# Output tiles in three parts, half-done products of w3 and w_out, a drain that can be split over two engines, and a new written order (attention and maxout FFN, one core)

## The chip, the core and the metric

The kernel runs on one core of one Trainium2 chip. The metric is the device time of one execution in microseconds; three runs of the kernel before gave 163.84, 164.56 and 164.87 us, the median is 164.56 us. The core has a tensor engine for matmuls (PE in the profile; PEld is its weight load), a vector engine (DVE), a scalar engine (ACT), GpSimd (POOL), and SyncE (SP), which here only issues output DMAs. Each engine runs its own instructions strictly in the order in which the program issued them; engines wait for one another by semaphores.

## What is computed

There are 8 batches of 8 heads, 576 rows and 64 columns a head; 32 memory slots per head. In short:

```python
a      = softmax(phi, axis=rows)                      # per head, 576 x 32
k_m    = a.T @ k ; v_m = a.T @ v                      # 32 x 64 per head
attn   = softmax(q @ k_m.T / 8, axis=slots)           # 576 x 32
x      = concat over heads of attn @ v_m              # 4608 x 512
h      = max(x @ w1, x @ w2, x @ w3)                  # 4608 x 768
out    = h @ w_out                                    # 4608 x 512, float32
```

## The kernel before, in words

The kernel never forms x. Per batch it folds the value slots into the weights: with d1 = w1 - w3 and d2 = w2 - w3, `h = x@w3 + max(x@d1, x@d2, 0)`, and since x = attn @ v_m, the products v_m @ d1, v_m @ d2 and v_m @ (w3 @ w_out) are made first (tile `wp`, 1536 columns, and tile `wp3`, 512 columns; line 433 and on, `fold`). Then `ffn1` (L461) makes attn @ wp in chunks of 128 hidden columns, and `ffn2` (L510) adds, for each output tile of 128 rows, six matmuls of hidden chunks against `w_out` (L532) and two matmuls of attn against wp3, the slots' values (L541; for t = 4, a tile of 64 rows of each of two batches, four half-size ones, L522).

All work is written out by hand: the string at L621 is a list of tokens `letter number @ batch`, and `issue` (L586) calls one function for each. An engine's queue is the order in which these tokens give it instructions. The letters that matter here:

- loads, all issued by POOL: L0 phi, L1 keys, L2 values, L3 queries of a batch; H0 to H3 the half loads of batch 0; Y0, Y1, Y2 the weights w1, w2, w3, and Y3 w_out. `r0`, `r1` pack keys and values side by side (POOL copies, L104); `G` makes POOL wait for a load.
- softmax over rows: E (ACT exponent), B (matmuls 64x32, L254), N (DVE, L274 to L288), K (transposes L303, then a drain). Batches 0 and 1 do keys and values apart (B0, B1 and so on).
- scores: Q (DVE transposes of q, L318, in two halves), S (matmuls 32x32, L338, then two ACT exponents, L347), then the softmax over slots on DVE and POOL: a (transpose L392), s (sum L400), c (reciprocal L409), m (POOL multiply L414), X (transpose back L422). Number 0 and 1 are two halves of the heads. Batch 0 does it with matmuls instead (M, R, X).
- D: fold, D0 D1 D2 the three column blocks of wp, D3 wp3; batch 0 has D0, D1, D2, D4, whose blocks differ (512, 256, 256 and 512 columns, `FIRST` at L211). V subtracts w3 from w1 and w2 in place on DVE (L219) once batch 0's folds have read them.
- F: even numbers are the d1 half of a chunk, drained with a relu to tile `h` (ACT L178 or DVE L182); odd ones are the d2 half, joined by a DVE max into tile `hT` (L484).
- P: the first three hidden matmuls of an output tile (`ffn2_head`, L495); T: the rest of it, its drain to tile `ot` and its output DMA.
- W, O: transposes of w3, and the rows of w3 @ w_out (six matmuls each, L200, drained to tile `w3o`). Z: matmuls on zeros that keep PE busy.

A drain is the copy of a finished PSUM result to SBUF. `evacuate` (L174) takes the engine from the table `EVAC` ("a" ACT, "v" DVE, by letter and number), and a `!` behind a token swaps it. PSUM is one tile of 8 banks; `one_bank` and `two_banks` (L156, L159) take the next digit of a second hand-written string (L149), which gives the first bank. A matmul into a bank waits until the bank's last reader is done.

Of the kernel before, what the change touches and what calls it, by code (L numbers as in the profile page):

```python
# [15 lines left out]
def kernel(  # L16
# [124 lines left out]
    for i in range(P // M):  # L141
# [4 lines left out]
    banks = iter(  # L146
        "".join(
            """
            60606026024506010445024062406246024602434403424206026420462406240723043240604602  # L149
            46026402645260502624620640264024601642102461462624604624260462045260024062404206  # L150
            12640264014206502402605220462406420462036040432402677670
            """.split()
        )
    )
# [1 line left out]
    def one_bank():  # L156
        return psum[:, int(next(banks))]
# [13 lines left out]

    EVAC = {"D": "avaaa", "T": "vavav", "K": "v", "W": "vvv", "O": "aaaa", "F": "aaaaaa"}

    def evacuate(kind, n, swap, out_, in_, relu=False):  # L174

        if (EVAC[kind][n] == "a") != swap:
            if relu:
                nc.scalar.activation(out=out_, in_=in_, func=AF.Relu)  # L178
            else:
                nc.scalar.copy(out=out_, in_=in_)  # L180
        elif relu:
            nc.vector.tensor_scalar_max(out=out_, in0=in_, scalar1=0.0)  # L182
        else:
            nc.vector.tensor_copy(out=out_, in_=in_)  # L184

    def w3_t(f2, swap):
# [7 lines left out]
                )  # L194
        evacuate("W", f2, swap, w3T[:, 2 * f2 : 2 * f2 + 2], pt)

    def w3_o(j, swap):
        po = one_bank()
        for f in range(FT):
            nc.tensor.matmul(  # L200
                po,
                lhsT=w3T[:, f, j, :],
                rhs=wo_sb[:, f, :],
                start=(f == 0),
                stop=(f == FT - 1),
            )
        evacuate("O", j, swap, w3o[:, j, :], po)
# [115 lines left out]
    attns = {}  # L323
# [168 lines left out]

    heads = {}

    def ffn2_head(b, t):  # L495

        hT = hts[b // 2]
        c0 = (b % 2) * (S + HP) + t * P
        po = heads[b, t] = one_bank()
        for n in range(HEAD):  # L500
            fc = fts[b][n]
            nc.tensor.matmul(  # L502
                po,
                lhsT=hT[:, fc, c0 : c0 + P],
                rhs=wo_sb[:, fc, :],
                start=(n == 0),
                stop=False,
            )

    def ffn2(b, t, swap):  # L510


        hT, attn = hts[b // 2], attns[b // 2]
        c0 = S - HP if t == 4 else (b % 2) * (S + HP) + t * P
        if b == B - 1 and t == 3:
            return ffn2_last(b, c0)
        po = heads[b, t] if (b, t) in heads else one_bank()

        if t == 4:
            for g in range(NG):  # L520
                for u in range(2):
                    nc.tensor.matmul(  # L522
                        po[HP * u : HP * (u + 1)],
                        lhsT=attn[:, g, c0 + HP * u : c0 + HP * (u + 1)],
                        rhs=wp3s[b - 1 + u][:, g, :],
                        start=(g == 0),
                        stop=False,
                        tile_position=(0, HP * u),
                    )
        for n in range(HEAD if (b, t) in heads else 0, FT):  # L530
            fc = fts[b][n]
            nc.tensor.matmul(  # L532
                po,
                lhsT=hT[:, fc, c0 : c0 + P],
                rhs=wo_sb[:, fc, :],
                start=(n == 0 and t < 4),
                stop=(n == FT - 1 and t == 4),
            )
        if t < 4:
            for g in range(NG):  # L540
                nc.tensor.matmul(  # L541
                    po,
                    lhsT=attn[:, g, c0 : c0 + P],
                    rhs=wp3s[b][:, g, :],
                    start=False,
                    stop=(g == NG - 1),
                )
        ot = opool.tile([P, DM], FP32, name="ot")
        r0 = (b // 2) * 2 * S + c0
        rows = out[r0 : r0 + P, :]  # L550
        evacuate("T", t, swap, ot, po)
        nc.sync.dma_start(out=rows, in_=ot)
# [66 lines left out]


    for w in """  # L621
        E@0 H0@0 H2@0 L3@0 Z25@0 B0@0 I@0 N0@0 Z2@0 K0@0! Q0@0 Q1@0 Z9@0 S@0 Z2@0 M0@0 M1@0
        R0@0 Y2@0 G0@0 R1@0 W0@0 Y3@0 W1@0 W2@0 Z6@0 O1@0 H3@0 O3@0 O2@0 H1@0 X1@0 B1@0 X0@0
        N1@0 K1@0 O0@0 Y0@0 D1@0! D0@0! D3@0 F8@0 F10@0 F2@0 V0@0 F6@0 F0@0! Y1@0 D2@0 L0@1
        V2@0 L1@1 D4@0 V1@0 L3@1 F4@0 F3@0 L2@1 L1@2 F1@0 L2@2 F7@0 F5@0 F9@0 F11@0 P0@0 E@1
        B0@1 N0@1 T3@0 K0@1! Q0@1 Q1@1 L0@2 T0@0! S@1 L3@2 P1@0 V4@0 B1@1 a0@1 T1@0 s0@1 L3@3
        N1@1 c0@1 L2@3 a1@1 s1@1 K1@1 c1@1 m0@1 P2@0 X0@1 D1@1 D0@1 m1@1 D2@1 X1@1 T2@0! L1@3
        r0@2 F2@1! F10@1 F0@1! F4@1 F8@1 F5@1 r1@2 F6@1 L0@3 E@2 F9@1 F11@1 L0@4 L1@4 F1@1 F7@1
        P2@1 F3@1 B@2 N@2 D3@1 P3@1 P0@1 K@2! Q0@2 Q1@2 T0@1! S@2 a0@2 s0@2 c0@2 T4@1! m0@2
        a1@2 s1@2 c1@2 T2@1! D2@2 Q1@3 D0@2 D1@2! T3@1 m1@2 T1@1 X1@2 r1@3 L3@4 L2@4 X0@2 L2@5  # L630
        Q0@3 F4@2 F6@2 F0@2 F8@2 F7@2 r0@3 F1@2 F10@2 F5@2 E@3 F9@2 F11@2 F2@2 B@3 D3@2 N@3
        F3@2 L0@5 P3@2 K@3 P0@2 L1@5 S@3 T0@2 a0@3 r0@4 s0@3 c0@3 a1@3 s1@3 P2@2 m0@3 c1@3 D2@3
        m1@3 D1@3! L3@5 D0@3 T3@2! Q1@4 X0@3 X1@3 T2@2! Q0@4 T1@2 F10@3! r1@4 F2@3 F11@3 F6@3
        F8@3! F3@3 E@4 F4@3 F9@3 F5@3 F0@3 F7@3 B@4 D3@3 N@4 F1@3 P1@3 K@4 L1@6 L0@6 T1@3! r1@5
        E@5 S@4 D2@4 L2@6 a0@4 T4@3! r0@5 s0@4 L0@7 a1@4 P0@3 D1@4! B@5 s1@4 c1@4 D0@4 L1@7
        c0@4 Q1@5 m1@4 T0@3! N@5 Q0@5 K@5 P2@3 L2@7 X1@4 m0@4 S@5 X0@4 T2@3! F0@4 F2@4 a0@5
        F4@4! F6@4 r1@6 a1@5 P3@3 L3@6 D1@5! r0@6 D3@4 s1@5 D3@5! T3@3 F10@4 s0@5 c1@5 F3@4
        F8@4 c0@5 F11@4 F1@4 F7@4 F5@4 F9@4 m0@5 P1@4 P0@4 E@6 D0@5 m1@5 X0@5 B@6 D2@5 X1@5
        T0@4 T1@4 N@6 F6@5 F0@5 F7@5 F1@5 F4@5! Q0@6 F2@5 r0@7 F10@5 r1@7 T3@4! Q1@6 F5@5 F8@5!
        E@7 K@6! F9@5 T2@4! F3@5 S@6 F11@5 a1@6 B@7 L3@7 D2@6 N@7 a0@6 D0@6 T4@5! s0@6 K@7 Q1@7  # L640
        P0@5 s1@6 D1@7! D3@7 c1@6 c0@6 D0@7 Q0@7 m1@6 T0@5! m0@6 P1@5 S@7 T1@5 X1@6 a0@7 a1@7
        P3@5 X0@6 D2@7 D1@6! s0@7 c0@7 D3@6 s1@7 T3@5! m0@7 c1@7 F6@6 P2@5 m1@7 X0@7 X1@7 F10@6
        T2@5! F7@6 F10@7! F4@6 F0@7! F11@6 F8@6 F11@7 F0@6! F2@6 F5@6 F1@6 F3@6 F2@7! P3@6 F9@6
        P2@6 F1@7 F6@7 F7@7 T2@6 F4@7! T3@6! F8@7 T0@6! T1@6 F9@7 F5@7 F3@7 P0@7 T1@7! T0@7
        T2@7 T4@7! T3@7
    """.split():
# [32 lines left out]
```

## Time and profile before

| What | us |
|---|---|
| median of 3 runs (lowest, highest) | 164.56 (163.84, 164.87) |
| profiled execution, its own time | 163.68 |
| its span in the profile | 161.9 |
| PE busy | 151.5 |
| DVE busy | 106.4 |
| ACT busy | 88.5 |
| POOL busy | 69.6 |

The granted TensorE clock is full throughout. The profiled execution is 0.88 us under the median of the three runs, and 1.78 us of its time lie outside the span. Busy time of PE counts each matmul's latency, in which others overlap; how fast matmuls follow one another is read from the chain of work, where 44 matmuls of 288 columns take 5.49 us and six of 512 columns 1.29 us.

### The profile page before, as it was taken

The page shows a single profiled execution, that of the slowest core. Times are in us where ns is not written, and L with a number is a line of the kernel's source. Part 1 is how long each engine was busy: PE and PEld are TensorE (multiplying, and loading weights), DVE is VectorE, ACT ScalarE, POOL GpSimd, SP SyncE. Part 2 cuts the span into 40 slices and gives each one's busy share as a digit, 9 for nine tenths or more (in the row PEclk, how much of TensorE's full clock was granted, in tenths as well). Part 3 has the DMA queues.
Part 4 walks back from the last instruction along what each step waited for, and adds up shares of the span by engine and source line. Part 5 has one row for each costly group of instructions (what it writes and reads, how often), then busy time and mean ns, then how long its engine had stood idle before and what let it go on. Part 6 is the DMA issues. An engine that isn't in the chain of part 4 may idle for free.

```text
span 161.9 us, 4816 instructions
## 1 busy us (share of the span) xinstructions
PE 151.5 (94%) x2056; PEld 85.6 (53%) x2080; DVE 106.4 (66%) x203; ACT 88.5 (55%) x129; POOL 69.6 (43%) x72
## 2 busy tenths in 40 slices
PE   7988799999899999999999999999999999999990
PEld 2443344664376436744774465656653467655450
DVE  2041704898969583959896959856897779863520
ACT  3206246926484769748567878477278963112010
POOL 7295213101879069746975914995004240000000
PEclk9999999999999999999999999999999999999999
DMA  5999999999999999999999999995911330024133
GB/s 152 176 203 201 203 211 214 276 208 208 260 312 236 208 244 382 282 212 215 314 278 208 292 287 306 235 208 140 188 72 65 130 112 21 0 84 158 74 143 132
DMA packets 21974, 31.77 MB, mean 196 GB/s; under 512 B 1216, under 2 KB 16576, under 8 KB 21952
## 3 DMA queue, kind: packets, MB, share of 16 engines
q0 software_dynamic: 16080, 21.43, 69.2%
q1 hardware_dynamic: 5728, 9.90, 17.4%
q8 instruction: 16, 0.26, 0.7%
q10 hardware_dynamic: 144, 0.13, 0.2%
q14 instruction: 6, 0.05, 0.1%
HBM read 39.32 MB, written 9.44 MB: 301 GB/s over the span
## 4 chain that ended last, share of the span: by engine, by line
PE 80%; DMA 10%; ACT 2%; issue 2%; DVE 2%; POOL 1%; ACTq 0%; POOLq 0%
PE psum L471 28%; PE psum L532 19%; PE psum L541 8%; PE psum L502 8%; DMA wo_sb<-in_moe_w_out_dram 7%; PE psum L445 6%; DMA kvo<-in_k_dram 4%; PE psum L254 4%; PE psum L200 3%; PE psum L338 2%; PE psum L522 1%; DVE sm L400 1%; PE psum L563 1%; ACT h L178 1%; PE psum L303 1%
## 5 line engine op out<-in xcount | busy, mean ns | idle before, releaser
L471 PE MATMUL psum<-attn,wp 128*128 128x288 bf16 x384 | 51.1, 286 | 0.1
L471 PEld LDWEIGHTS <-wp 128*128 128x128 bf16 x384 | 37.0, 98 | 14.1 <-issue 1.1
L484 DVE TENSOR_TENSOR hT<-psum,h 128x576 bf16<-128x576 f32 x48 | 34.2, 751 | 10.8 <-PE psum L471 9.8
L532 PE MATMUL psum<-wo_sb,hT 128*128 128x512 bf16 x131 | 34.1, 380 | 1.5 <-issue 1.4
L180 ACT CAST wp<-psum 128x1024 bf16<-128x1024 f32 (+1 forms) x30 | 28.2, 991 | 9.0 <-PE psum L445 7.2
L104 POOL COPY kvr<-kvo 128x2304 bf16<-128x2304 bf16 x12 | 25.3, 2112 | 10.5 <-PE psum L541 5.8
L178 ACT ACTIVATE h<-psum 128x576 bf16<-128x576 f32 x35 | 21.7, 661 | 14.3 <-PE psum L471 14.1
L180 ACT COPY ot<-psum 128x512 f32<-128x512 f32 x24 | 14.2, 596 | 22.8 <-PE psum L541 13.6
L414 POOL TENSOR_TENSOR t<-t,sm 128x576 bf16<-128x576 bf16 x14 | 16.1, 1155 | 22.7 <-DVE sm L409 22.4
L532 PEld LDWEIGHTS <-hT 128*128 128x128 bf16 x144 | 12.6, 98 | 16.7 <-issue 5.3
L541 PE MATMUL psum<-wp,attn 128*128 128x512 bf16 x62 | 18.4, 379 | 0.1
L502 PE MATMUL psum<-wo_sb,hT 128*128 128x512 bf16 x58 | 16.8, 379 | 0.5 <-issue 0.2
L167 PE MATMUL psum<-warm 128*128 128x512 bf16 x42 | 12.2, 447 | 1.4 <-DVE warm L136 1.2
L347 ACT ACTIVATE e<-psum 128x576 bf16<-128x576 f32 x16 | 9.6, 657 | 5.7 <-PE psum L338 5.7
L318 DVE STREAM_TRANSPOSE qT<-qq 128x576 f32<-128x576 f32 x16 | 11.8, 750 | 0.8 <-DMA qq<-in_q_dram 0.8
L182 DVE TENSOR_SCALAR h<-psum 128x576 bf16<-128x576 f32 x13 | 9.8, 752 | 3.2 <-PE psum L471 1.9
L111 POOL DMA_DIRECT2D qq<-in_q_dram x8 | 6.2, 774 | 12.8 <-DVE qT L318 7.6
L184 DVE COPY ot<-psum 128x512 f32<-128x512 f32 x11 | 7.5, 681 | 6.4 <-PE psum L541 4.4
L234 ACT ACTIVATE e<-ph 128x1152 bf16<-128x1152 f32 (+1 forms) x9 | 9.5, 1056 | 2.2 <-DMA ph<-in_phi_dram 2.2
L400 DVE TENSOR_REDUCE sm<-t 128x18 f32<-128x576 bf16 x14 | 10.4, 742 | 0.3
L541 PEld LDWEIGHTS <-attn 128*128 128x128 bf16 x62 | 6.1, 98 | 7.2
L98 POOL DMA_DIRECT2D kvo<-in_v_dram x9 | 6.7, 744 | 7.0 <-PE psum L254 4.0
(61 smaller groups left out, 135.5 us busy)
## 6 DMA issues: line engine op xcount, KB each, us to landing
out_dram<-ot SPq DMA_DIRECT2D x35, 256.0 KB, 5.4
qq<-in_q_dram POOLq DMA_DIRECT2D x8, 576.0 KB, 12.2
ph<-in_phi_dram POOLq DMA_DIRECT2D x7, 576.0 KB, 15.3
kvo<-in_k_dram POOLq DMA_DIRECT2D x7, 576.0 KB, 18.5
kvo<-in_v_dram POOLq DMA_DIRECT2D x7, 576.0 KB, 16.9
w_sb<-in_moe_w_dram POOLq DMA_DIRECT2D x3, 768.0 KB, 15.1
wo_sb<-in_moe_w_out_dram POOLq DMA_DIRECT2D x1, 768.0 KB, 10.7
ph<-in_phi_dram SPq DMA_DIRECT2D x2, 288.0 KB, 3.1
```

Of the source, the lines that this page charges most:

```text
L104: nc.gpsimd.tensor_copy(out=kvrs[b % 2][:, :, :, D * i : D * (i + 1)], in_=kvos[b % 2][:, 1 - i])
L167: nc.tensor.matmul(po[:, 0:BANK], lhsT=warm[:, 0:P], rhs=warm, start=True, stop=True)
L178: nc.scalar.activation(out=out_, in_=in_, func=AF.Relu)
L180: nc.scalar.copy(out=out_, in_=in_)
L318: nc.vector.transpose(out=s["qT"][:, j].rearrange("p j c r e -> p (j c r e)").bitcast(FP32), in_=loaded[b]["q"][:, j].rearrange("p j c d - ...
L400: nc.vector.tensor_reduce(out=sm, in_=s["t", g].rearrange("p n r e -> p n e r"), op=ALU.add, axis=mybir.AxisListType.X,)
L414: nc.gpsimd.tensor_tensor(out=t, in0=t, in1=s["sm", g].unsqueeze(2).to_broadcast([P, S // HP, R, 2]), op=ALU.mult,)
L471: nc.tensor.matmul(acc[:, h, 0:SH], lhsT=wps[b][:, g, w * DF + ft * P : w * DF + (ft + 1) * P], rhs=attn[:, g, c0 : c0 + SH], start=(g == ...
L484: nc.vector.tensor_tensor(out=hT[:, ft, (b % 2) * S : (b % 2 + 1) * S].rearrange("p (h n) -> p h n", h=2), in0=a, in1=s["h1", ft], op=ALU.max,
L502: nc.tensor.matmul(po, lhsT=hT[:, fc, c0 : c0 + P], rhs=wo_sb[:, fc, :], start=(n == 0), stop=False,)
L532: nc.tensor.matmul(po, lhsT=hT[:, fc, c0 : c0 + P], rhs=wo_sb[:, fc, :], start=(n == 0 and t < 4), stop=(n == FT - 1 and t == 4),)
L541: nc.tensor.matmul(po, lhsT=attn[:, g, c0 : c0 + P], rhs=wp3s[b][:, g, :], start=False, stop=(g == NG - 1),)
```

## The change

- `evacuate` gets a suffix `how` in place of a flag. A `^` in it splits a two-bank drain: one bank goes to the engine of the table, the other to the other engine. The new order has no token with a `^`; the call at its end strips and passes such a suffix.
- `w3_o_head` (token J) issues the first three of the six matmuls of an O token earlier and leaves the bank open; O then does what is left. J3, J2 and J1 are used.
- `ffn2` is cut up: `ffn2_slots` (new token p) does the two matmuls of the slots' values, `ffn2_hidden` (token P, three chunks) hidden ones, and T whatever is left, hidden before slots' values unless these are done. An output tile may be begun by either. Before, the slots' values always came last (t < 4). The matmuls are the same in number and shape; 30 tokens are added (3 J, 23 p, 4 P) and seven P tokens taken out.
- The order from R0@0 on and the bank string are new. POOL's first 17 loads keep their order; behind them L1@3 and L0@3 come before r0@2, and r0@3 and r1@4 stand ahead of m0@2 and m0@3.
- The engine of 37 drains changes. Of folds (D) ACT has 23 instead of 30 and DVE 10 instead of 3; of relu drains (F) ACT 28 instead of 35 and DVE 20 instead of 13; of output tiles (T) ACT 24 and DVE 12 instead of 25 and 11; of O, ACT 2 and DVE 2 instead of 4 and 0; of K, ACT 6 and DVE 4 instead of 4 and 6.

The diff, without the old order and the old banks:

```diff
--- before.py
+++ after.py
@@ -146,9 +146,9 @@
     banks = iter(
         "".join(
             """
...
+            60606026024506015204024062460240264126424522622206026420460426047201240642162064
+            20642046274026204632464064264024062045024610264306406406064026401246426246024604
+            62406272046022047042614206426466402640742042426043044370
             """.split()
         )
     )
@@ -171,7 +171,16 @@
 
     EVAC = {"D": "avaaa", "T": "vavav", "K": "v", "W": "vvv", "O": "aaaa", "F": "aaaaaa"}
 
-    def evacuate(kind, n, swap, out_, in_, relu=False):
+    def evacuate(kind, n, how, out_, in_, relu=False):
+
+        swap = "!" in how
+        if "^" in how:
+            first = "" if EVAC[kind][n] == "a" else "!"
+            second = "!" if EVAC[kind][n] == "a" else ""
+            x = 1 if kind == "D" and swap else 0
+            evacuate(kind, n, first, out_[:, x], in_[:, x], relu)
+            evacuate(kind, n, second, out_[:, 1 - x], in_[:, 1 - x], relu)
+            return
 
         if (EVAC[kind][n] == "a") != swap:
             if relu:
@@ -194,9 +203,24 @@
                 )
         evacuate("W", f2, swap, w3T[:, 2 * f2 : 2 * f2 + 2], pt)
 
+    w3_heads = {}
+
+    def w3_o_head(j):
+        po = one_bank()
+        for f in range(HEAD):
+            nc.tensor.matmul(
+                po,
+                lhsT=w3T[:, f, j, :],
+                rhs=wo_sb[:, f, :],
+                start=(f == 0),
+                stop=False,
+            )
+        w3_heads[j] = po, HEAD
+
     def w3_o(j, swap):
-        po = one_bank()
-        for f in range(FT):
+        po, done = w3_heads.pop(j, (None, 0))
+        po = one_bank() if po is None else po
+        for f in range(done, FT):
             nc.tensor.matmul(
                 po,
                 lhsT=w3T[:, f, j, :],
@@ -492,32 +516,19 @@
 
     heads = {}
 
-    def ffn2_head(b, t):
-
-        hT = hts[b // 2]
-        c0 = (b % 2) * (S + HP) + t * P
-        po = heads[b, t] = one_bank()
-        for n in range(HEAD):
-            fc = fts[b][n]
-            nc.tensor.matmul(
-                po,
-                lhsT=hT[:, fc, c0 : c0 + P],
-                rhs=wo_sb[:, fc, :],
-                start=(n == 0),
-                stop=False,
-            )
-
-    def ffn2(b, t, swap):
-
-
-        hT, attn = hts[b // 2], attns[b // 2]
+    def tile_parts(b, t):
+
         c0 = S - HP if t == 4 else (b % 2) * (S + HP) + t * P
-        if b == B - 1 and t == 3:
-            return ffn2_last(b, c0)
-        po = heads[b, t] if (b, t) in heads else one_bank()
-
-        if t == 4:
-            for g in range(NG):
+        po, done = heads.get((b, t)) or (one_bank(), set())
+        heads[b, t] = po, done
+        return po, done, c0
+
+    def ffn2_slots(b, t, last=False):
+
+        po, done, c0 = tile_parts(b, t)
+        attn = attns[b // 2]
+        for g in range(NG):
+            if t == 4:
                 for u in range(2):
                     nc.tensor.matmul(
                         po[HP * u : HP * (u + 1)],
@@ -527,24 +538,43 @@
                         stop=False,
                         tile_position=(0, HP * u),
                     )
-        for n in range(HEAD if (b, t) in heads else 0, FT):
+            else:
+                nc.tensor.matmul(
+                    po,
+                    lhsT=attn[:, g, c0 : c0 + P],
+                    rhs=wp3s[b][:, g, :],
+                    start=(g == 0 and not done),
+                    stop=(last and g == NG - 1),
+                )
+        done.add("slots")
+
+    def ffn2_hidden(b, t, ns, last=False):
+
+        po, done, c0 = tile_parts(b, t)
+        hT = hts[b // 2]
+        for n in ns:
             fc = fts[b][n]
             nc.tensor.matmul(
                 po,
                 lhsT=hT[:, fc, c0 : c0 + P],
                 rhs=wo_sb[:, fc, :],
-                start=(n == 0 and t < 4),
-                stop=(n == FT - 1 and t == 4),
-            )
-        if t < 4:
-            for g in range(NG):
-                nc.tensor.matmul(
-                    po,
-                    lhsT=attn[:, g, c0 : c0 + P],
-                    rhs=wp3s[b][:, g, :],
-                    start=False,
-                    stop=(g == NG - 1),
-                )
+                start=(n == ns[0] and not done),
+                stop=(last and n == ns[-1]),
+            )
+        done.update(ns)
+
+    def ffn2(b, t, swap):
+
+        if b == B - 1 and t == 3:
+            return ffn2_last(b, S + HP + t * P)
+        po, done, c0 = tile_parts(b, t)
+        if t == 4 and "slots" not in done:
+            ffn2_slots(b, t)
+        first = "slots" in done
+        left = [n for n in range(FT) if n not in done]
+        ffn2_hidden(b, t, left, last=first)
+        if not first:
+            ffn2_slots(b, t, last=True)
         ot = opool.tile([P, DM], FP32, name="ot")
         r0 = (b // 2) * 2 * S + c0
         rows = out[r0 : r0 + P, :]
@@ -608,7 +638,9 @@
             "R": lambda: ones_rec(b, i),
             "D": lambda: fold(b, i, swap),
             "F": lambda: ffn1(b, i, swap),
-            "P": lambda: ffn2_head(b, i),
+            "P": lambda: ffn2_hidden(b, i, range(HEAD)),
+            "p": lambda: ffn2_slots(b, i),
+            "J": lambda: w3_o_head(i),
             "T": lambda: ffn2(b, i, swap),
             "W": lambda: w3_t(i, swap),
             "O": lambda: w3_o(i, swap),
@@ -620,32 +652,33 @@
 
     for w in """
         E@0 H0@0 H2@0 L3@0 Z25@0 B0@0 I@0 N0@0 Z2@0 K0@0! Q0@0 Q1@0 Z9@0 S@0 Z2@0 M0@0 M1@0
...
+        R0@0 Y2@0 G0@0 R1@0 W0@0 Y3@0 W1@0 W2@0 H3@0 H1@0 Z6@0 O0@0 J3@0 Y0@0 X0@0 J2@0 Y1@0
+        B1@0 L0@1 N1@0 J1@0 L1@1 L3@1 X1@0 L2@1 K1@0 O1@0! O3@0 O2@0! D1@0! D0@0! D3@0! F8@0
+        V0@0 F10@0 L1@2 F2@0 V1@0 F6@0 F4@0! F0@0! D2@0 V2@0 D4@0 E@1 p3@0 F1@0 F3@0 L2@2 F5@0
+        p0@0 F11@0 F7@0 P3@0 L0@2 F9@0 B0@1 T3@0 N0@1 Q1@1 p1@0 Q0@1 p2@0 K0@1! L3@2 P0@0 S@1
+        V4@0 L1@3 T0@0! a0@1 B1@1 s0@1 N1@1 P1@0 L0@3 c0@1 K1@1! a1@1 P2@0 s1@1 c1@1 m0@1 X0@1
+        m1@1 r0@2 r1@2 D0@1 D2@1 X1@1 L2@3 L3@3 D1@1! r0@3 T2@0 T1@0 F0@1! L2@4 F4@1 F10@1!
+        F8@1 F9@1 F6@1 F2@1! F1@1 F7@1 E@2 F3@1 F5@1 P3@1 B@2 N@2 D3@1 Q0@2 P2@1 F11@1 K@2!
+        p2@1 p1@1 T2@1! p3@1 Q1@2 S@2 a0@2 s0@2 c0@2 L1@4 a1@2 s1@2 m0@2 c1@2 m1@2 r1@3 L0@4
+        L3@4 r1@4 T3@1 T1@1 T0@1 E@3 X0@2 D0@2! L1@5 X1@2 D2@2 D1@2! T4@1! F4@2 Q0@3 F10@2 F5@2
+        F11@2 F8@2 B@3 N@3 D3@2 r0@4 F9@2 Q1@3 F0@2 F2@2 F6@2 F3@2 K@3 F1@2 P2@2 L3@5 S@3 p2@2
+        L2@5 F7@2 a0@3 s0@3 E@4 L0@5 a1@3 p1@2 c0@3 T1@2 s1@3 T2@2! m0@3 D2@3! c1@3 D3@3 B@4
+        Q1@4 D0@3 m1@3 L1@6 N@4 Q0@4 p3@2 T0@2! K@4! P3@2 X1@3 L0@6 X0@3 D1@3 r0@5 S@4 L2@6
+        T3@2! F8@3! F2@3 a0@4 F0@3 s0@4 F9@3 F10@3! c0@4 F4@3 F3@3 F5@3 F6@3 L1@7 L3@6 F1@3
+        F11@3 a1@4 F7@3 m0@4 Q1@5 p1@3 s1@4 P1@3 Q0@5 E@5 T3@3 T1@3 c1@4 D1@4 r1@5 B@5 D2@4
+        D0@4! m1@4 T4@3! N@5 X1@4 K@5 X0@4 r0@6 P0@3 S@5 a0@5 a1@5 s0@5 P2@3 F2@4 L3@7 F0@4!
+        L0@7 p0@3 E@6 F4@4! c0@5 F10@4 r1@6 p2@3 s1@5 F1@4 F11@4 m0@5 F8@4 T2@3! F3@4 F9@4 c1@5
+        r0@7 T0@3! F6@4! D3@4 m1@5 D1@5 B@6 N@6 D2@5 X0@5 D0@5 p2@4 P2@4 X1@5 Q0@6 p1@4 F5@4
+        F7@4 F2@5! Q1@6 T1@4 K@6! F6@5 L2@7 F0@5 T2@4! S@6 F8@5! F1@5 F9@5 F10@5! Q0@7 F3@5
+        F11@5 a1@6 E@7 T0@4! D3@5 r1@7 B@7 N@7 D1@6! D2@6 P3@4 a0@6 p3@4 Q1@7 F4@5 s0@6 c0@6
+        T3@4 P0@5 K@7 m0@6 F7@5 s1@6 F5@5 P3@5 X0@6 S@7 c1@6 a0@7 p3@5 a1@7 s1@7 m1@6 c1@7
+        T0@5! T3@5! X1@6 D0@6 D3@7 s0@7 m1@7 D0@7! T4@5! F0@6! D3@6 c0@7 D2@7! D1@7! p1@5 X1@7
+        m0@7 X0@7 P1@5 F10@6 F11@6 p2@5 F4@6 F5@6 F1@6 F2@6 T1@5 F6@6! F8@6! T2@5 F6@7! F3@6
+        F7@6 F0@7! P3@6 F2@7! F9@6 P1@6 F8@7 F10@7 F9@7 p3@6 F4@7! F7@7 T3@6! F3@7 p2@6 p0@6
+        F5@7 F11@7 p0@7 P0@7 F1@7 T4@7 T2@6 T1@7! T0@7! T1@6! T2@7 T0@6 T3@7
     """.split():
-        n, b = w.rstrip("!").split("@")
-        issue(int(b), n, w.endswith("!"))
+        n, b = w.rstrip("!^").split("@")
+        issue(int(b), n, w[len(n) + 1 + len(b) :])
 
 
 # ---- launch: one core; inputs and outputs as the reference has them ----
```

More of the change, by code (lines that the diff above doesn't have):

```diff
@@ L148 @@
             """
-            60606026024506010445024062406246024602434403424206026420462406240723043240604602
-            46026402645260502624620640264024601642102461462624604624260462045260024062404206
-            12640264014206502402605220462406420462036040432402677670
+            60606026024506015204024062460240264126424522622206026420460426047201240642162064
+            20642046274026204632464064264024062045024610264306406406064026401246426246024604
+            62406272046022047042614206426466402640742042426043044370
             """.split()
@@ L622 @@
         E@0 H0@0 H2@0 L3@0 Z25@0 B0@0 I@0 N0@0 Z2@0 K0@0! Q0@0 Q1@0 Z9@0 S@0 Z2@0 M0@0 M1@0
[L623 to L645, printed above, removed]
+        R0@0 Y2@0 G0@0 R1@0 W0@0 Y3@0 W1@0 W2@0 H3@0 H1@0 Z6@0 O0@0 J3@0 Y0@0 X0@0 J2@0 Y1@0
```

## The prediction

> **What bounds the kernel now.** I read the page first, then the list of what PE waited for, the groups kept apart by shape, the timeline of the drains in the lead, and the chain of waits.
>
> ```profile
> PE 151.5 (94%) x2056; PEld 85.6 (53%) x2080; DVE 106.4 (66%) x203; ACT 88.5 (55%) x129; POOL 69.6 (43%) x72
> PEclk9999999999999999999999999999999999999999
> L484 DVE TENSOR_TENSOR hT<-psum,h 128x576 bf16<-128x576 f32 x48 | 34.2, 751 | 10.8 <-PE psum L471 9.8
> L178 ACT ACTIVATE h<-psum 128x576 bf16<-128x576 f32 x35 | 21.7, 661 | 14.3 <-PE psum L471 14.1
> L182 DVE TENSOR_SCALAR h<-psum 128x576 bf16<-128x576 f32 x13 | 9.8, 752 | 3.2 <-PE psum L471 1.9
> ```
>
> PE is busy nearly throughout at full clock; DVE and ACT have idle time, mostly waiting for PE. The groups by shape give the price of a fold's drain on each engine, the waits of PE what it still lacks, and the two windows what DVE carries where it is fullest.
>
> ```profile
> L180 ACT CAST wp<-psum 128x1024 bf16<-128x1024 f32 x28 | 27.1, 1020 | 9.0 <-PE psum L445 7.2 <-DVE rden L274 1.8
> L184 DVE CAST wp<-psum 128x1024 bf16<-128x1024 f32 x3 | 3.7, 1225 | 1.9 <-PE psum L445 1.9
> PE psum L200 <- DMA wo_sb<-in_moe_w_out_dram: 1.0, 1, 1.0
> PE psum L445 <- DVE kvt L184: 0.3, 1, 0.3
> 75.00:107.00 32.00, 31.37 (x515) 18.58 (x519) 26.64 (x52) 23.02 (x32) 23.05 (x20) 1.00 1.16 268
> 27.00:44.00 17.00, 16.14 (x317) 9.40 (x313) 15.58 (x27) 10.04 (x17) 4.50 (x6) 1.00 1.18 235
> ```
>
> The window rows give PE, PEld, DVE, ACT and POOL busy, clock, DMA share and GB/s. DVE is 83% busy from 75 to 107 and 92% in the lead from 27 to 44, yet PE hardly waits. The lead on DVE:
>
> ```profile
> 26.87 1.23 DVE L184 CAST wp<-psum 128x1024 bf16<-128x1024 f32 x1 [1.88 <-PE psum L445]
> 28.01 1.22 DVE L219 TENSOR_TENSOR w_sb<-w_sb 128x2048 bf16<-128x2048 bf16 x1
> 29.92 0.76 DVE L182 TENSOR_SCALAR h<-psum 128x576 bf16<-128x576 f32 x1 [0.69 <-ACT h L178]
> 30.60 1.28 DVE L219 TENSOR_TENSOR w_sb<-w_sb 128x1024 bf16<-128x1024 bf16 x2
> 31.89 4.08 DVE L484 TENSOR_TENSOR hT<-psum,h 128x576 bf16<-128x576 f32 x6
> 26.54 1.65 ACT L180 CAST wp<-psum 128x512 bf16<-128x512 f32 x2
> ```
>
> From 26.87 to 36 DVE has one gap (0.69). Here D0 is drained by DVE, D1 and D3 by ACT (last row, the names of its first shape). Six maxes take 4.08, so 0.68 each where they follow one another, against 0.75 alone; DVE's busy 106.4 is likewise 0.944 of the 112.7 that its rows would sum to. I use that factor for stretches.
>
> **PE's own work does not change.** From the chain of waits, a 512-column matmul follows the last after 0.215 us (six in 1.29) and a 288-column one after 0.1225. Summing the tokens from F8@0 to T3@7 gives 122.8 us in either order. Each run of small-tile tokens (B, S, D, T4's slots) costs PE some 0.2 to 0.35 us of switching (24 matmuls of D, three banks, take 0.77 for 0.65 of streaming, and 0.09 on entry). Behind F8@0 there are 23 such runs before, 21 in the new order: two entries, **-0.2**. The seven P tokens taken out, the 23 p and four P added only move matmuls; a tile begun early holds a bank, no time of its own. The `^` branch is never called, since no token has one: nothing for it, though the words for the change say 27 drains. SP's DMAs stay one a tile and hang on T. The tail keeps T3@7 last, in halves: nothing.
>
> **The w3 products.** w_out's load lands at about 19.2 (issued 8.49, 10.7 to landing) and the same 17 loads go first on POOL, so nothing starts earlier there. w1 lands at 25.8 (issued 10.71, 15.1 to landing), and D1@0 started at 25.95. The 24 matmuls need 5.2 us from 19.35; with B1 between, PE is done by 25.5 in the new order too and waits for w1. J splits change nothing. But D1's drain on ACT (26.54) stood behind O0's (26.06 to 26.64); O0's is now long done, O1's and O2's are on DVE. F8@0 can start near 26.9 in place of 27.19: **-0.3**.
>
> **DVE's queue in the lead.** DVE now gets O2 (0.68), D0 (1.23), D3 (1.23, ACT before), V0 (1.2), V1 (0.65), F4 (0.75, ACT before), F0 (0.75), then V2, in that order and from about 26.65. Back to back, D3's drain ends at 29.1. F6@0 takes D3's banks 4 and 5; PE, after F8, F10 and F2, is there at 28.4: wait 0.7. F0's drain then ends at 32.1 to 32.4; p3@0 takes its bank 0, and PE is there at 31.6 (D2 and D4 having started after w2's landing at 29.8, unchanged): wait 0.6. The six maxes start 1.7 later than before, so F9's ends at 37.8 and T3@0's last hidden matmul waits 0.4. N0, Q1 and Q0 stand behind the maxes, so S@1 waits 0.2; B1@1 waits 0.2 for the exponent that frees S's bank; K1 0.1 for N1; F0@1's second half 0.4 for X1, which follows S by the chain a, s, c, m (measured 39.85 to 44.96 in the timeline before). Sum 2.6. What goes with it are PE's own waits of that stretch: 0.12 for w2, 0.15 for v of batch 1 and 0.36 for K1's drain, with smaller ones 0.9 by the stretch's length. Net **+1.7**, so F of batch 1 starts at about 46.05, against 44.66, the -0.3 included.
>
> **Batch 1 to F4@2.** In F@1 DVE drains F0, F10, F2 and T2, and ACT the three folds in a row (3 x 1.02), with F4 and F8 behind them. F9, F2 and F7 end late, P3@1 waits for F7's max and T2@1 for F11's: 0.4. At F4@2, X1@2 stands on DVE behind T0@1 (0.68) and D0@2 (1.23, ACT before), so PE waits 0.2 for it. **+0.6.** POOL's early r0@3 must wait for batch 3's keys; the transfers are a queue that was full before (DMA share 1.1 to 1.2), so I take them at about 55.7, the place of the next load behind batch 2's queries. r0@3 (2.11), L2@4 and L1@4 then end at 59.3, just when m0@2 can start (c0@2 at 59.5): nothing, bounded by 0 and the 2.1 of one pack.
>
> **Batches 3 to 5, where DVE runs out.** Over all, DVE takes 7 folds (1.225), 7 relus (0.752), two O and a T (0.68) and gives two K (0.347): +15.2 by rows. ACT falls by 12.6. From D1@3's drain to N@5, DVE's rows sum to 15.9, times 0.944 is 15.0; PE streams 13.6 in that stretch up to K@5, which needs N@5. DVE starts it with 0.2 of lag: PE loses 1.6, at F8@3 (for D1@3's drain), F5@3 (for F10's bank), K@5. From there to T1@4, which needs F7@4's max, DVE has 14.2 and 0.9 of waiting for S@5's exponent, PE 14.8: another 0.4. **+2.0.** Behind it DVE is below PE again (stretches of 4 us of PE hold 3 to 4.8), and a PE that waited doesn't catch up.
>
> By the Trainium skill (Perfetto Trace Analysis, Optimizing Scalar/DVE Operations) a VectorE instruction on PSUM has about 125 ns of access overhead and its profiled latency holds twice that, half of which overlaps the next instruction. By that estimate the first stretch would be 13.9 in place of 15.0, and the whole change about +2.4. The six maxes show 0.08 of overlap each, so I stay with the factor.
>
> **Sum:** -0.2 - 0.3 + 1.7 + 0.6 + 2.0 = +3.8; half of the small waits of before behind 44.66 (0.46 by the length of the stretch) may not recur, so I take **+3.5**. That is 163.68 + 3.5 = 167.2 for the profiled execution, which was 0.9 under the median; as the median, 164.56 + 3.5, rounded, **168.0**.
>
> **Rivals.**
> 1. *The banks absorb it.* By the same sums of rows DVE lagged PE by some 2.4 us near 42 to 45 before, with only 0.36 of wait. The order can let drains be late by as much; then only -0.5 and F6 and p3 (+1.3), less 0.9, are left: 164.5. Against: F6 and p3 wait for one named drain each, and from D1@3 on the lag is never paid back. Chance 0.14.
> 2. *Faster.* The waits of PE from 19.35 on (0.4 for N1, 0.24 for O0's drain ahead of D3, 0.9 behind F8) all go, and no new one comes, since tiles begun early give PE other work: -1.7 with the entries, 162.8. It decides at F6@0: if D3's drain ends before 28.4 it can hold. For it: p and P tokens stand at places of such waits. Against: D0 and D3 are queued on one engine. Chance 0.07.
> 3. *POOL and the loads add to it.* r0@3 and r1@4 hold POOL until their loads land, with m0@2, m1@2 and m0@3 and further loads behind them; X and F wait. Q1@4 stands ahead of N@4 on DVE and needs batch 4's queries, which landed at about 74.2 before with fewer loads ahead; I get 76.5 against 76.2 for DVE. One pack late (2.1) and a pair of loads late (1.1): 168.0 + 3.2 = 171.2. Chance 0.17.
> 4. *The split drains do happen* (27 of them, half of each on ACT): DVE back near its 106 busy, as rival 1: 164.5. The diff speaks against it. Chance 0.03.
>
> **How the numbers follow.** My case 0.59 (166 to 170), rivals 0.14, 0.07, 0.17, 0.03. A measurement can tell about 1% (1.65 us) from no change. Slower by over 1%: cases 0 and 3, less the low end of mine, 0.76 + 0.02 of rival 1 = 0.78. Within 1%: 0.15. Faster: 0.07. The range leaves out rival 2 and most of 1 below and the end of rival 3 above: 164.8 to 171.2.
>
> **What would show it.** Right: DVE busy about 120, ACT about 76; in the timeline F6@0 after D3's drain near 29.1 and p3@0 after F0's near 32.2; first F of batch 1 near 46; DVE without gaps from 80 to 95; PE's waits naming drains L184 and L182 and N's kvn, not DMAs. Wrong: F of batch 1 by 45, DVE idle before L484 in batch 3, or waits on loads in their place.

## The result, and the profile after

| What | before | after |
|---|---|---|
| median of six runs of each kernel (lowest, highest), us | 164.18 (163.84, 164.87) | 169.06 (168.27, 170.11) |
| profiled execution, us | 163.68 | 169.25 |
| its span, us | 161.9 | 167.5 |
| DVE busy, us | 106.4 | 119.0 |
| ACT busy, us | 88.5 | 77.3 |

The six runs of before include the three named ahead of the prediction. The change makes the kernel slower: ratio 1.0295, interval 1.0254 to 1.0336, by 4.9 us. The page of after, first the busy times, then the groups of the drains:

```profile
PE 154.7 (92%) x2080; PEld 85.9 (51%) x2080; DVE 119.0 (71%) x218; ACT 77.3 (46%) x114; POOL 69.6 (42%) x72
L508 DVE TENSOR_TENSOR hT<-psum,h 128x576 bf16<-128x576 f32 x48 | 34.5, 748 | 7.7 <-PE psum L495 6.0
L187 ACT ACTIVATE h<-psum 128x576 bf16<-128x576 f32 x28 | 17.4, 653 | 15.5 <-PE psum L495 15.2
L191 DVE TENSOR_SCALAR h<-psum 128x576 bf16<-128x576 f32 x20 | 14.7, 752 | 3.6 <-PE psum L495 3.4
L193 DVE CAST wp<-psum 128x1024 bf16<-128x1024 f32 x10 | 12.0, 1212 | 1.3 <-PE psum L469 1.3
```

The granted clock is full as before (the page's PEclk row shows nines throughout), and one drain costs what it cost before on either engine (a fold on DVE 1.21 us, a relu 0.75); there are only more of them on DVE: 10 folds for 3, 20 relus for 13. ACT gave up what DVE took, and idles. PE's waits have changed owners. What PE waited for in after (total, times, longest, in us):

```profile
PE psum L495 <- DVE wp L193: 0.7, 2, 0.5
PE psum L542 <- DVE h L191: 0.7, 1, 0.7
PE psum L542 <- DVE wp L193: 0.6, 1, 0.6
PE psum L495 <- DVE h L191: 0.4, 1, 0.4
PE psum L557 <- DVE h L191: 0.4, 1, 0.4
```

Each names a drain by DVE (L193 a fold, L191 a relu) in front of PE: F (L495), slots' values (L542), hidden products (L557). In before the largest wait of that kind was 0.3. The windows of after, with the columns of those of before:

```profile
75.00:107.00 32.00, 30.49 (x515) 17.67 (x514) 29.28 (x55) 18.03 (x27) 24.75 (x22) 1.00 1.16 256
27.00:44.00 17.00, 15.73 (x323) 9.20 (x324) 15.49 (x25) 8.17 (x13) 2.98 (x4) 1.00 1.19 226
```

From 75 to 107 DVE is busy for 29.28 of 32 us (before 26.64) and PE for 30.49 (before 31.37). DMA share, 1.16, is what it was. From 27 to 44 DVE's busy time is what it was (15.49, before 15.58), while PE's falls from 16.14 to 15.73.

Token by token, the 5.6 us between the two profiled executions divide as follows. All starts are of PE, from the timeline.

| Stretch | before | after | difference |
|---|---|---|---|
| to the landing of w1 | 25.80 | 26.91 | +1.1 |
| from there to F8@0 | 1.39 | 1.25 | -0.1 |
| F8@0 to the first F of batch 1 | 17.47 | 18.96 | +1.5 |
| from there to F4@2 | 17.36 | 17.28 | -0.1 |
| F4@2 to T3@7 | 94.3 | 97.5 | +3.2 |

The first line isn't the change's: w1 landed anywhere between 25.8 and 26.9 in the executions of this study with the same loads ahead of it (26.08 in another execution of before, 25.96 in one of the new order; the mean is 26.2 of the three traces in the old order and 26.4 of the nine in the new one). Without it 4.5 us are left, close to the 4.9 of the medians.

### The profile page after: what moved, and what is told of

Read it like the earlier page. It is cut to its first block, busy times and chain, and to the rows that moved or that the text cites. A ratio compares the mean times of both kernels' runs of the same rounds, so it can differ in the third digit from the quotient of the medians.

```text
span 167.5 us, 4838 instructions
## 1 busy us (share of the span) xinstructions
PE 154.7 (92%) x2080; PEld 85.9 (51%) x2080; DVE 119.0 (71%) x218; ACT 77.3 (46%) x114; POOL 69.6 (42%) x72
## 4 chain that ended last, share of the span: by engine, by line
PE 65%; DMA 13%; DVE 12%; issue 3%; ACT 2%; POOL 2%; DVEq 0%; POOLq 0%
PE psum L495 26%; PE psum L557 24%; DMA w_sb<-in_moe_w_dram 9%; PE psum L542 8%; DVE wp L193 4%; DMA kvo<-in_k_dram 4%; PE psum L469 2%; DVE sm L424 2%; DVE h L191 2%; ACT wp L189 2%; PE psum L278 2%; POOL kvo L98 1%; DVE hT L508 1%; PE psum L362 1%; PE psum L533 1%
## 5 line engine op out<-in xcount | busy, mean ns | idle before, releaser
L495 PE MATMUL psum<-attn,wp 128*128 128x288 bf16 x384 | 52.9, 286 | 1.4 <-DVE wp L193 0.7
L557 PE MATMUL psum<-wo_sb,hT 128*128 128x512 bf16 x210 | 52.8, 380 | 0.5 <-DVE h L191 0.4
L495 PEld LDWEIGHTS <-wp 128*128 128x128 bf16 x384 | 36.9, 98 | 17.5 <-issue 2.3
L557 PEld LDWEIGHTS <-hT 128*128 128x128 bf16 x210 | 19.4, 98 | 22.5 <-issue 4.1
L189 ACT COPY ot<-psum 128x512 f32<-128x512 f32 x23 | 13.4, 588 | 29.0 <-PE psum L557 23.0
L189 ACT CAST wp<-psum 128x1024 bf16<-128x1024 f32 (+1 forms) x23 | 21.5, 981 | 7.4 <-PE psum L469 7.4
L187 ACT ACTIVATE h<-psum 128x576 bf16<-128x576 f32 x28 | 17.4, 653 | 15.5 <-PE psum L495 15.2
L542 PE MATMUL psum<-wp,attn 128*128 128x512 bf16 x62 | 18.1, 379 | 1.4 <-DVE h L191 0.7
L191 DVE TENSOR_SCALAR h<-psum 128x576 bf16<-128x576 f32 x20 | 14.7, 752 | 3.6 <-PE psum L495 3.4
L193 DVE CAST wp<-psum 128x1024 bf16<-128x1024 f32 x10 | 12.0, 1212 | 1.3 <-PE psum L469 1.3
L193 DVE COPY ot<-psum 128x512 f32<-128x512 f32 x12 | 8.2, 686 | 5.9 <-PE psum L542 3.1
L98 POOL DMA_DIRECT2D kvo<-in_k_dram x9 | 6.9, 771 | 9.2 <-PE psum L278 7.1
L542 PEld LDWEIGHTS <-attn 128*128 128x128 bf16 x62 | 5.8, 97 | 7.2 <-issue 3.2
L278 PEld LDWEIGHTS <-e 64*32 64x32 bf16 x720 | 7.2, 90 | 3.4 <-issue 2.2
```

Source lines behind the costliest of these rows:

```text
L495: nc.tensor.matmul(acc[:, h, 0:SH], lhsT=wps[b][:, g, w * DF + ft * P : w * DF + (ft + 1) * P], rhs=attn[:, g, c0 : c0 + SH], start=(g == ...
L542: nc.tensor.matmul(po, lhsT=attn[:, g, c0 : c0 + P], rhs=wp3s[b][:, g, :], start=(g == 0 and not done), stop=(last and g == NG - 1),)
L557: nc.tensor.matmul(po, lhsT=hT[:, fc, c0 : c0 + P], rhs=wo_sb[:, fc, :], start=(n == ns[0] and not done), stop=(last and n == ns[-1]),)
```

## The experiments

In the short diffs "..." stands for the rest of the order. Unless something else is said, an experiment starts from the changed kernel. The first four ran together, beside the kernel before at 164.45 us; e5 to e8 together, beside it at 164.5; e9 to e11 together, beside it at 164.38. An interval is that of the ratio to the kernel before.

**e1: split the drains for real.** The words for the change say that 27 drains are shared; the diff has no `^`. Here 27 of the drains that DVE has get one.

```diff
-... D0@0! D3@0! F8@0 ... F6@0 F4@0! F0@0! ...
+... D0@0!^ D3@0!^ F8@0 ... F6@0 F4@0!^ F0@0!^ ...
```

> The changed kernel with a ^ on 27 of the 30 folds and relu drains that VectorE has (all but F0, F2 and F4 of batch 7), so that each is split, one bank on either engine. Theory (VectorE's queue of whole drains holds banks and PE waits for them): VectorE falls from 119.0 to about 108 us busy, ScalarE rises from 77.3 to about 90; the waits of PE at F6@0, p3@0, F8@3, F5@3, T4@3, p2@4 and T0@4 shrink by more than half, and the time is 163.5 to 166. Rival (the new order or the parts of output tiles make it slow): it stays within 1 us of the changed kernel, 168 to 170.

Measured: 168.39 us, 1.0238 (1.0187 to 1.0289). DVE is back at 110.1 us, and of the waits listed for after, those for DVE's drains are gone. The time is not. In their place stand loads. From e1's timelines of DVE, PE and ACT:

```profile
66.61 0.78 DVE L342 STREAM_TRANSPOSE qT<-qq 128x576 f32<-128x576 f32 x1 [3.19 <-DMA qq<-in_q_dram]
67.32 1.38 DVE L508 TENSOR_TENSOR hT<-psum,h 128x576 bf16<-128x576 f32 x2
...
68.09 0.41 PE L469 MATMUL psum<-w3o,kvt 64*32 64x512 bf16 x8 [1.19 <-DVE hT L508]
...
92.70 1.16 ACT L258 ACTIVATE e<-ph 128x1152 bf16<-128x1152 f32 x1 [5.04 <-DMA ph<-in_phi_dram]
...
93.91 0.80 PE L278 MATMUL psum<-kvr,e 64*32 64x129 bf16 x72 [1.74 <-ACT e L258]
```

The bracket behind an instruction is the engine's idle time ahead of it and what ended it. DVE stands still for 3.19 us at Q0@3, until the queries of batch 3 land; two maxes are queued behind it, and D3@2 needs the bank of one of them (PE loses 1.19). ACT stands still for 5.04 us until phi of batch 5 lands, and B@5 waits 1.74 for its exponent. My theory's time was missed and the rival's came out. The trace is of the slowest of e1's four executions (169.37 us; the fastest took 167.38).

That loads come late here is the new order's doing in part. It gives three of them another place in POOL's queue of loads (all in us; "used" is the start of the first instruction that reads the load):

| Load | before: asked, landed, used | after: asked, landed, used |
|---|---|---|
| queries of batch 3 | 38.67, 55.67, 59.17 | 51.48, 64.00, 64.37 |
| phi of batch 4 | 50.90, 67.32, 80.33 | 65.08, 74.22, 74.30 |
| phi of batch 5 | 67.72, 83.03, 85.08 | 76.21, 91.09, 91.11 |

The last of the twelve loads of batches 3 to 5 lands at 89.73 in before and at 91.09 in after, so the queue as a whole delivers nearly as fast. But these three land 7 to 8 us later than they did, and phi of batch 4 is wanted 6 us earlier than before. So the rival, the order, has a part in it. No run put the loads back in their old places.

**e2 and e3: order and engines apart.** e2 is the new order with each drain on the engine that it had before; e3 the old order with the new engines (a `!` toggled on 37 tokens each).

```diff
-... O1@0! O3@0 O2@0! D1@0! D0@0! D3@0! ... F4@0! ...
+... O1@0 O3@0 O2@0 D1@0! D0@0! D3@0 ... F4@0 ...
```

> The changed kernel's order, parts and banks, but every drain on the engine that it had before (37 changed back). Theory: VectorE back at about 106 us busy, so most waits of PE go; the order was written for other drains, so ScalarE may be late in places; 164 to 166.5. Rival (order and parts): 168 to 170.

Measured: 170.5 us, 1.0368 (1.0340 to 1.0396): missed, and slower than the whole change. The timelines of ACT and PE in e2:

```profile
62.88 2.83 ACT L189 CAST wp<-psum 128x1024 bf16<-128x1024 f32 x3
...
65.76 1.45 PE L495 MATMUL psum<-attn,wp 128*128 128x288 bf16 x10 [1.16 <-ACT wp L189]
```

At the head of batch 2 three folds now stand in a row on ACT, and F10@2 waits for the last of their banks. In after, one of the three is on DVE.

> The order and banks of before, with the engine of each drain as in the changed kernel (37 changed). Theory: VectorE at about 119 us busy holds banks in this order too; F6@0 waits for D3's drain as in the changed kernel; 167 to 170. Rival (order and parts): within 1 us of the kernel before, 163.5 to 165.2.

Measured: 175.7 us, 1.0684 (1.0622 to 1.0746): the direction was the theory's, the size was underrated. Of what PE waited for in e3, the largest:

```profile
PE psum L303 <- DVE kvn L278: 4.2, 2, 2.6
```

K waits for N on DVE twice: K1@0 1.64 us, where N stands behind a drain of O and the two X of batch 0, and K@5 2.59 us, where it stands behind two folds, a sum and a transpose of q. So engines and order can't be judged apart: each of the two crossings is slower than either kernel.

**e4: the early packs later.** r0@3 and r1@4 go back behind the POOL multiplies (m) that feed the X of the batch before.

```diff
-... D1@1! r0@3 T2@0 ... m1@2 r1@3 L0@4 L3@4 r1@4 ... m0@3 ...
+... D1@1! T2@0 ... m1@2 r0@3 r1@3 L0@4 L3@4 ... m0@3 r1@4 ...
```

> The changed kernel with two packs later on GpSimd: r0@3 behind m1@2 and r1@4 behind m0@3. Theory (VectorE): the multiplies were not late, so within 0.6 us of the changed kernel, 168.3 to 169.6. Rival (GpSimd blocked by early packs makes X late and adds to the loss): 1 to 3 us faster than the changed kernel, 166 to 168.

Measured: 174.83 us, 1.0629 (1.0602 to 1.0656). Both expectations missed it: B@4 waits 4.74 us in one go for r1@4, since in the new order B@4 comes some 7 us earlier than in the old one (at 76.0 in after, 83.1 in before). The timelines of POOL and PE in e4:

```profile
78.15 2.13 POOL L104 COPY kvr<-kvo 128x2304 bf16<-128x2304 bf16 x1
...
80.34 1.18 PE L278 MATMUL psum<-kvr,e 64*32 64x129 bf16 x72 [4.74 <-POOL kvr L104]
```

The first F of batch 1 to the first of batch 2 took 17.29 us here, 17.28 in after: r0@3 in its early place costs the X of batch 2 nothing. r1@4 in its early place is what B@4 needs.

**e5, e6, e7: the loads lightened.** 17 of the 35 whole-tile output transfers are left unwritten, in the changed kernel with split drains (e5), in the changed kernel (e6) and in the kernel before (e7).

```diff
-            nc.sync.dma_start(out=rows, in_=ot)
+            if b >= 5 or t == 0:
+                nc.sync.dma_start(out=rows, in_=ot)
```

> The split drains of e1_share27, and 17 of the 35 whole-tile output transfers left out (every tile but t = 0 of batches 0 to 4, so these rows of the output are not written), which gives the loads room. Theory now (two limits lie close together, VectorE's whole drains and the loads; with the drains split the kernel waits for queries of batch 3 and phi of batch 5 instead): both waits, 1.9 and 2.4 us, go, 163.5 to 165.5. Rival (the order itself is slow for another reason): 167 or more.

> The changed kernel with the same 17 output transfers left out. Theory: its waits are VectorE's, the loads are just in time behind them; 167.5 to 169, at most 1.5 us under the changed kernel. Rival (loads alone make the loss): 164 to 165.5, as e5_share_fewer_outputs.

> The kernel before with the same 17 output transfers left out. Both theories: it hardly waits for loads behind the lead, so 163.4 to 164.8; if it gains as much as e5_share_fewer_outputs does over e1_share27, the gain there is no sign of the new order's loads.

Measured: e5 164.64 us, 1.0001 (0.9972 to 1.0030); e6 168.6, 1.0231 (1.0169 to 1.0293); e7 164.3, 0.9977 (0.9944 to 1.0010). All three are inside what the theory gave. One of e7's ten executions, the profiled one, took 866.73 us, and its trace is not read. The same window of e5, then of e6, then of e1:

```profile
75.00:107.00 32.00, 31.90 (x522) 19.05 (x498) 27.64 (x60) 22.55 (x37) 22.93 (x19) 1.00 0.99 203
```

```profile
75.00:107.00 32.00, 30.38 (x522) 17.74 (x507) 29.25 (x55) 18.04 (x26) 23.20 (x19) 1.00 0.94 198
```

```profile
75.00:107.00 32.00, 30.11 (x461) 17.37 (x462) 26.00 (x55) 21.21 (x36) 24.63 (x22) 1.00 1.17 250
```

In e6 the DMA share falls to 0.94 and DVE stays at 29.25: PE waits as in after. In e1 DVE falls to 26.00 and the DMA share stays at 1.17: PE waits too, for loads. Only in e5, with both lightened, is PE busy for 31.90 of 32 us. The loads do land earlier there: the queries of batch 3 at 61.23 and phi of batch 5 at 82.94, against 66.59 and 92.67 in e1. The other way in which fewer outputs could help, drains that wait for a free `ot` buffer, is not there: in the lists of waits of after and of e1 no drain waits for an output transfer. Put together:

| | all output transfers | fewer |
|---|---|---|
| changed kernel | 169.06 | e6: 168.6 |
| with its drains split | e1: 168.39 | e5: 164.64 |
| kernel before | 164.18 to 164.5 | e7: 164.3 |

Taking away one limit in this table brings 0.5 to 0.7 us, which these intervals don't tell from nothing; taking away both brings 4.4. (e10 below, which splits 13 drains in place of 27, does bring 1.4 alone.) The kernel before gains nothing from fewer output transfers.

**e8: split drains, loads asked for in time.** It starts from e1, and all work is done. The transposes that stuck are moved behind what they held up, and phi of batch 5 is loaded ahead of its values and queries.

```diff
-... F4@2 Q0@3 F10@2 ... r0@4 F9@2 Q1@3 ... L3@5 S@3 p2@2 L2@5 ... E@4 L0@5 ... m0@4 Q1@5 p1@3 s1@4 P1@3 Q0@5 E@5 ... X0@4 r0@6 ...
+... F4@2 F10@2 ... r0@4 F9@2 Q0@3 Q1@3 ... L0@5 S@3 p2@2 L2@5 ... E@4 L3@5 ... m0@4 p1@3 s1@4 P1@3 E@5 ... X0@4 Q1@5 Q0@5 r0@6 ...
```

> e1_share27 with the two waits for loads moved out of the way, all work done: Q0 of batch 3 behind F9 of batch 2, phi of batch 5 loaded before its values and queries, and Q1 and Q0 of batch 5 behind X0 of batch 4. Theory (loads): the waits at D3 of batch 2 (1.9) and at B of batch 5 (2.4) shrink by more than half, 165 to 167. Rival: no change from e1_share27, 167.4 to 169.4.

Measured: 168.28 us, 1.0206 (1.0153 to 1.0258): missed. The waits for queries of batch 3 and phi of batch 5 are gone, and others stand there. PE's timeline in e8:

```profile
75.84 0.80 PE L278 MATMUL psum<-kvr,e 64*32 64x129 bf16 x72 [1.13 <-ACT e L258]
...
97.07 0.48 PE L362 MATMUL psum<-qT,kvt 32*32 32x288 bf16 x32 [1.57 <-DVE qT L342]
```

The first is B@4, whose exponent waited for phi of batch 4: phi of batch 4 lands at 74.54, no later than in after (74.22), but PE is there earlier. The second is S@5, and it is no wait for a load: the queries of batch 5 had landed at 90.56, and the transposes start at 95.62 since I had moved them behind X0@4. So e8 made a loss of its own, and it does not settle what the loads alone cost.

**e9: only the lead repaired.** D3@0 and F4@0 go back to ACT.

```diff
-... D0@0! D3@0! F8@0 ... F4@0! F0@0! ...
+... D0@0! D3@0 F8@0 ... F4@0 F0@0! ...
```

> The changed kernel with only D3 and F4 of batch 0 back on ScalarE. Theory: the waits of PE at F6@0 (0.64) and p3@0 (0.88) go, so the first F of batch 1 starts 17.4 to 17.9 us behind F8@0 instead of 18.96; but the loads of batches 3 and 5 were just in time, so less than that is left at the end: 168.0 to 169.1. Rival (VectorE alone sets the time): the whole 1.3 us is left, 167.4 to 167.9.

Measured: 169.55 us, 1.0318 (1.0268 to 1.0368): missed, since nothing is left at the end. The lead did gain: F8@0 to the first F of batch 1 took 17.92 us in place of 18.96. But then D3@2 starts 0.49 us later behind the token ahead of it than in after and F9@2 0.29 (DVE stands at the queries of batch 3), B@4 0.25, B@5 with D2@4 0.80 (phi of batch 5), and K@5 loses 0.28. These queries landed at 65.14 (64.00 in after) and phi of batch 5 at 91.39 (91.09): a microsecond won ahead of loads that come no earlier was waited away behind them.

**e10: only the middle split.** Thirteen drains of batches 3 to 5 get a `^`.

```diff
-... D2@3! ... D1@3 ... F8@3! ... F10@3! ... D1@4 ... D0@4! ... F0@4! ... F4@4! ... F6@4! ... D1@5 ... F2@5! ... F8@5! ... F10@5! ...
+... D2@3!^ ... D1@3^ ... F8@3!^ ... F10@3!^ ... D1@4^ ... D0@4!^ ... F0@4!^ ... F4@4!^ ... F6@4!^ ... D1@5^ ... F2@5!^ ... F8@5!^ ... F10@5!^ ...
```

> The changed kernel with a ^ on the 13 folds and relu drains that VectorE has in batches 3 to 5, the lead as in the changed kernel. Theory: the waits at p3@2, F8@3, F5@3, T4@3 and T0@4 (2.8 us in all) shrink by more than half, and waits for loads (phi of batch 5 above all) come in their place; 168 to 169.2. Rival (VectorE alone): 166 to 167.

Measured: 167.69 us, 1.0201 (1.0171 to 1.0231), between the theory's time and the rival's. This interval lies under that of the change, so the 1.4 us are a gain. The waits of F8@3, F5@3, T4@3 and T0@4 are gone, that of p3@2 has shrunk from 0.82 to 0.31. B@5 waits again, 0.43, for the exponent in this line of ACT's timeline in e10, and D2@4 behind it 0.37, for the drain of an output tile that stands behind the exponent on ACT:

```profile
90.50 1.16 ACT L258 ACTIVATE e<-ph 128x1152 bf16<-128x1152 f32 x1 [3.54 <-DMA ph<-in_phi_dram]
```

**e11: the kernel before once more**, for the spread of one landing.

> The kernel before once more, for a second trace: where w1 lands (25.8 us in the first, 25.96 to 26.9 in the traces of the other kernels) and when F8@0 starts. All theories: the landing moves from execution to execution, 25.5 to 27, F8@0 1.4 behind it, and the time is 163.7 to 165.

Measured: 163.85 us. w1 lands at 26.08 (25.80 in the execution first shown) and F8@0 starts 1.41 later (1.39).

## Why the prediction was right, and where it was not

The forecast of 168.0 us (164.8 to 171.2, slower with a chance of 0.78) came out at 169.06. The cause that it put first, whole drains queued on DVE that hold banks, is shown by the list of waits, and by e6 against e5: with the loads lightened, splitting these drains takes 168.6 to 164.64. That a second limit of the same size lies right behind it was not foreseen. The time was met in part by luck, since a term that failed (+0.6) and one that came out too small (+2.0) made up for each other in part.

**The lead, +1.7: right in its two large waits, +1.5.** The two waits that it named are in PE's timeline of after:

```profile
28.16 1.74 PE L495 MATMUL psum<-attn,wp 128*128 128x288 bf16 x12
30.36 1.63 PE L495 MATMUL psum<-attn,wp 128*128 128x288 bf16 x12 [0.46 <-DVE wp L193]
...
33.43 0.59 PE L542 MATMUL psum<-wp,attn 128*128 128x512 bf16 x2 [0.66 <-DVE h L191]
```

and the queue that makes them in DVE's:

```profile
27.95 2.36 DVE L193 CAST wp<-psum 128x1024 bf16<-128x1024 f32 x2 [0.51 <-PE psum L469]
...
31.96 1.42 DVE L191 TENSOR_SCALAR h<-psum 128x576 bf16<-128x576 f32 x2
...
34.60 4.23 DVE L508 TENSOR_TENSOR hT<-psum,h 128x576 bf16<-128x576 f32 x6 [0.63 <-PE psum L495]
```

D0 and D3 come back to back (2.36), and F6@0 starts when D3's banks are free: PE loses 0.64 between the streaming of the two groups, of which the bracket counts 0.46 (0.7 predicted). The second wait is p3@0 behind F0's drain: 0.88 (0.6). With w1's landing, 1.1 later than in before, taken off, the two drains end at 29.2 and 32.3, as forecast (29.1, 32.1 to 32.4), and the first F of batch 1 starts at 46.0 (46.05). F0@1 waits 0.38 (0.4), but that is luck: not X1 ended this wait but a fold's drain on ACT. The smaller waits named at T3@0 (0.4) and S@1 (0.2) did not come, and fewer of before's own waits went than I took off. e9 puts D3 and F4 on ACT: F6's wait goes, and p3@0's shrinks to 0.36.

**The start of F8@0, -0.3: -0.1** (1.25 us behind w1's landing in place of 1.39). PE stands 0.3 us at the landing, so J's early products brought nothing, as predicted.

**Batch 1 to F4@2, +0.6: failed, -0.1.** I took P3@1, T2@1 and X1@2 to wait; none did. Of the three folds in a row on ACT one held F0@1, in the line above; behind that they were in time. The step about r0@3, costed at nothing, holds (e4).

**Batches 3 to 5, +2.0: the mis-sized term.** From F4@2 to the end it is +3.2, where I had the 2.0 less the small waits of before that don't recur. The waits of F8@3 (0.42), F5@3 (0.54) and T4@3 (0.48), and of the slots' values p2@4 (0.29), lie where DVE was said to run out and name its drains; K@5, named too, did not wait. Others behind DVE had not been named: p3@2 (0.82), whose bank D2@3's drain holds; T0@4 (0.53, F10@5's drain) and D3@6 (0.39). D0@5 (0.27) and P3@4 (0.38) wait for folds on ACT, and these two waits are still there in e5, with DVE's drains split. The chain of waits in after shows waits behind DVE's drains (start, us, what):

```profile
76.48 1.14 DVE wp L193
...
77.67 0.59 PE psum L542 x2
...
81.28 1.24 DVE wp L193
...
82.56 3.16 PE psum L495 x24
...
85.78 0.76 DVE h L191
...
86.58 2.61 PE psum L495 x20
```

Three times in 10 us the chain leaves PE for one whole drain of DVE. DVE's share of the chain of the whole span is 12% (2% before). What failed in the working: I set sums of DVE's rows against sums of PE's over two stretches, and so saw a backlog only where the sum ran over. A whole drain that comes late in DVE's queue can cost PE 0.3 to 0.8 us in a stretch in which DVE as a whole keeps up. The factor was off as well: the rows of before, count times mean, sum to 115.5 and not to 112.7, so it is 0.92; with it the first stretch gives about 14.6 in place of 15.0, and +1.2 in place of +1.6 (F8@3, F5@3 and T4@3 lost 1.4).

**Busy times: right.** DVE 119.0 (about 120 predicted), ACT 77.3 (about 76).

**The rivals.** I gave the banks that absorb it, the loads, and drains that are split as alternatives. The table of the changed kernel, e1, e5 and e6 shows that two of them hold at once: in after the loads land just in time behind DVE's delays, and with the drains split they no longer do. ACT's timeline in after shows how near it is: ACT idles 2.65 us for phi of batch 5, and its exponent is done half a us before B@5 (92.80).

```profile
91.11 1.16 ACT L258 ACTIVATE e<-ph 128x1152 bf16<-128x1152 f32 x1 [2.65 <-DMA ph<-in_phi_dram]
```

Rival 3 named the loads, but as a delay on top; in after lightening them gains only 0.5 us (e6), since DVE's delays come first. Rival 4's price was wrong as well: I put the split drains at 164.5, since DVE would be back near its 106; they take 168.39, and 164.64 only with fewer output transfers. And a sum of waits, one stretch after another, is not what the end shows: e9 takes one us out of the lead and the time stays.

**The rule on overlapping instructions.** The two folds above take 2.36 us for twice 1.21: 0.06 to 0.07 of overlap. Over all 61 pairs in after in which one instruction of DVE that reads PSUM starts before the last such one ends, the median overlap is 0.083. By the Trainium skill (Perfetto Trace Analysis, Optimizing Scalar/DVE Operations) some 125 ns would overlap; the estimate by it, +2.4, lies further from the measured 4.9 than the sum by the rows, so the measured overlap decides. The same section of the Trainium skill says that it may make sense to move work to ScalarE where DVE is saturated: here splitting 27 drains with ScalarE gave 0.7 us by itself, no more than the interval, with loads standing right behind; with these lightened it gave 4.0 (168.6 to 164.64).

**Left open.** Why the split of thirteen drains (e10, 167.36 to 168.27) seems to do better than that of 27 (e1, 167.38 to 169.37) wasn't settled. The two traces differ at the queries of batch 3: e1 wins 0.8 us in the lead and loses 1.7 at D3@2 and F9@2 until they land (66.59), e10 leaves the lead as it is and loses 0.3 there (65.33). With one trace of each, the order's part and the spread of a landing can't be told apart. What of e2's and e3's losses is order and what is late loads was not taken apart further. No version tried beats the kernel before: even with both limits gone the parts of tiles, the early products and the new order bring 164.64, against 164.3.

## What to carry to other kernels

Here an engine that was 83% busy in a stretch could not be given whole two-bank drains for nothing: what counted was not its sum but how long each drain held its bank. So set every moved drain against the next matmul into its banks. When taking away the visible wait changes little, look for a second limit just behind it and take both away in one run; two limits of nearly equal size can each look worth little alone (0.5 and 0.7 us here, of 4.4). An order that needs a load earlier than another (B@4 by 7 us here), or asks for it later (phi of batch 4 by 14 us), spends the slack that had hidden it.

## What the runs showed of the hardware

The same load, asked for at the same place in the queue, landed up to 1.1 us apart: w1 at 25.80, 25.96, 26.08, 26.52, 26.68, 26.74 and 26.91 in seven executions, and between these in the other five whose traces were read. It was issued between 10.71 and 12.14, but that does not order the landings: the one that landed last (26.91) was issued at 11.17. The first of the 16 DMA engines is done with it at nearly the same time (24.55 to 24.97); the last one is 1.1 us behind the first in the earliest of these executions and 2.3 us in the latest. That is as much as some of the terms predicted here, so a single profiled execution shouldn't settle a difference of one us that lies behind a load.
